# A block-causal attention and gated-MLP kernel: the same program with the work of every engine put in another order

## The chip, the cores and the metric

The kernel runs on one core of a Trainium2 chip, in one launch. The metric is the device time of that launch in microseconds: the median of 3 runs before the change, beside one profiled execution of its own. Engines are named as in the profile: PE is TensorE's matmul (PEld its weight load), DVE VectorE, ACT ScalarE, POOL GpSimd, SP the SyncE queue, which here issues the loads and the regrouping transfers.

## The reference

Attention on 8 images, 8 heads, 576 tokens, head size 64, with a mask that lets a block of 64 tokens see itself and all blocks before it. The heads side by side (512 wide) go through a gated MLP: a projection to 1024 with ReLU, one half normalised per token and mixed over the tokens by a 576 x 576 matrix, multiplied with the other half, and projected to 512.

```python
def _attn_ref(q, k, v):                       # q, k, v: 8, 8, 576, 64
    scores = scale * np.matmul(q, k.transpose(0, 1, 3, 2))
    mask = block_i >= block_j                 # blocks of 64 tokens
    scores = np.where(mask, scores, -1000000000.0)
    scores = scores - np.max(scores, axis=-1, keepdims=True)
    attn = np.exp(scores)
    attn = attn / (np.sum(attn, axis=-1, keepdims=True) + 1e-09)
    return np.matmul(attn, v).astype(np.float32)

def _moe_ref(x, w_in, w_spatial, b_spatial, w_out):   # x: 8, 576, 512
    h = np.maximum(x @ w_in, 0.0)
    u, v = (h[..., :d_ff // 2], h[..., d_ff // 2:])   # 512 each
    v_n = (v - mu) / np.sqrt(var + 1e-06)             # per token
    v_s = np.einsum('ts,bsd->btd', w_spatial, v_n) + b_spatial[None, :, None]
    gated = u * v_s
    return (gated @ w_out).astype(np.float32)
```

## The kernel before

**The program as a list.** The whole program is a string of step words, `ORDER` (line 46 on). A word such as `a.5*2` names a kind of step, its numbers and how often it is taken. `step()` advances the generator of that step until it has issued at least one instruction, and `in_order()` then chains each new instruction behind the last one of its engine. So the string alone sets the order on every engine and on the SP queue; semaphores between engines only follow from the data.

**Attention.** The 8 images have 4 head pairs each, 32 pairs `g` in all; image `b` needs pairs 4b to 4b+3. `load.g` brings queries and keys of a pair into one of two `raw` buffers (576 KB, L373), `loadv.g` the values into one of two `v` buffers. For pairs 4 to 31: `s.g` are the score products (L801 by 512 columns, into three PSUM banks and one shared one, each freed when DVE has read it at L593), `8.g` those of the last 64 rows (L619), `n.g` the softmax's scaling on POOL (L695) and DVE, `t.g` 8 groups of 32 x 32 block transposes on DVE (L849, L839), which fill a buffer `pb`. `r.g` and `r8.g` are four DMA issues each on SP that regroup `pb` into `ptt` (L877, 320 KB; L869, 80 KB). `a.g` is attention times values (L894, L906), ended by evacuations on ACT and DVE (L506, L508) into `x`. Pairs 0 to 3, and a part of pair 4, go another way at the start (`set`, `ns`, `ts`, `alo`, `ahi`: L735 and L763 scores, transposes on TensorE at L453, products at L532 to L558).

**MLP of image b.** `v.b.*` are the products for the mixed half (L947, L959), `u.b.*` for the other half (L1030, evacuated by ACT at L1036), `g.b.*` the token mixing (L1082, L1086, L1087), ended by the multiplication with u on DVE (L1090), and `o.b.*` the last projection, cut into smaller products whose sums DVE and ACT add up (L1162; L1170, L1174 and L1183). These groups share two PSUM banks (pool `ps_m`): a group starts when the evacuation of the one two before it has ended.

**Weights** are fetched on SP and decoded into two parts while pairs 0 to 7 run: `w.k` (512 KB from L238; decode on DVE at L256, L265, L280 and on ACT) and `sw.c` (the token-mixing matrix, 288 KB each at L336). The tail of the program is the MLP of image 7, with no attention left beside it.

Of the kernel before, what the change touches and what calls it, by code (L numbers as in the profile page):

```python
# [47 lines left out]
set.4*2 set.3 ns.3 set.4 ts.1*4 w.0 ns.3 w.0 w.2*2 w.0 set.4 ns.4*2 w.2 w.0 loadv.0 alo.0*2
ts.2*4 set.5 sw.1 set.5 sw.2*4 ts.3*4 set.5*2 set.6 set.5 set.6*4 w.0*2 set.7 alo.0 set.7*2
w.2*2 ns.5*3 set.7*2 ns.6*3 ahi.0 set.7*4 load.2 set.8*3 ts.4*2 ts.5*2 ahi.0 set.8 ns.7*3  # L50
set.10*4 ts.5*2 w.3 ahi.0 ns.7 ts.6*4 set.9*5 ahi.0*2 ts.4*2 w.3*2 ns.8 ts.7*2 ns.7 ts.7*2 w.2*2
ns.8 set.10 ns.9*3 set.11*7 loadv.1 ahi.1*3 set.11*2 ns.10*3 w.3*4 load.3 set.12*2 ahi.1*2 ts.8
pad ts.8 set.12*2 ts.9 sw.0*4 alo.1 ts.9 ts.10*2 set.14*2 w.4*2 ns.11*3 alo.1*2 ts.9*2 ts.10*2
ns.12*2 ts.8*2 set.13 w.4 set.13*4 ns.11*2 w.4 set.14*2 w.5*2 set.14 w.5 loadv.2 ahi.2*3 ns.13*3
w.6*2 set.15*3 ts.11*4 w.5*2 ns.14*3 w.4*2 ahi.2*3 ts.12*4 set.15*6 w.5*2 load.4 set.16 ts.13*2
alo.2*2 ts.13*2 loadv.3 set.16*2 ts.14*4 alo.2 set.16*3 w.4 ns.15*5 sw.4 load.5 set.17*4
set.18*2 ns.16*3 w.6*5 ahi.3*2 set.17 ts.15*3 set.19 ahi.3 ts.15 set.18*2 ahi.1 set.18 set.19*2
alo.3*2 8.5 ns.17*3 sw.1*3 ahi.3*3 w.7 set.19*3 ns.18 set.19*3 alo.3 v.0.0*2 ns.18 sw.4*3 t8.4*2
ns.19*4 t.4*2 v.0.0*2 8.5*2 v.0.1*2 w.8*3 loadv.4 w.7*2 t.4*2 ns.19 v.0.1*2 v.0.2*2 ns.18 t.4*3
ahi.0 t.4 sw.4*2 v.0.0*4 v.0.1*3 w.8 v.0.1 w.7*2 v.0.2*2 v.0.3*2 8.5 w.8*4 8.5*2 v.0.2*3  # L60
u.0.1.0*2 w.7*2 v.0.3*2 s.5 load.6 s.5*9 r8.4 8.5 n.5*2 v.0.4*2 w.9 v.0.3 8.5*2 s.5*5 n.5*4
s.5*2 v.0.4*2 u.0.1.1*2 v.0.2 t8.5*2 n.5 t.5*2 r.4 w.9*4 v.0.4*2 n.5 a.4 n.5*3 t.5*6 a.4*3 w.9*2
8.6*3 u.0.1.3 u.0.0.1*2 sw.3*2 w.9*4 8.6 v.0.3*3 w.9*2 u.0.1.3 a.4*2 w.10*3 u.0.0.0*2 u.0.0.3*2
v.0.4*2 sw.3*2 s.6*4 8.6*2 v.0.4 r8.5 s.6*2 v.0.4*2 loadv.5 w.9*2 u.0.1.2*2 8.6*3 s.6*6 w.10*2
w.9*3 g.0.0.0*4 n.6*3 s.6*5 u.0.0.2*2 t8.6*2 load.7 8.7*3 n.6*8 r.5 a.5*4 w.10*3 t.6*8 w.11*6
loadv.6 g.0.0.1*2 g.0.0.2*2 8.7*3 w.11*3 a.5*2 g.0.0.1*2 w.11*2 g.0.1.1*3 8.7*3 w.11*3 s.7*8
n.7*3 r8.6 g.0.0.3 load.8 8.8 s.7*9 w.11*2 n.7*5 w.11 split.8*2 n.7*3 g.0.0.3 g.0.1.0*4 r.6
a.6*4 t8.7*2 loadv.7 t.7*3 w.11 t.7*5 g.0.1.3*4 split.8 g.0.1.2*3 g.0.1.0*3 g.0.1.1*4 g.0.1.3
a.6 g.0.1.3*2 load.9 g.0.1.3 8.8*4 o.0.0.1*2 a.6 8.8 r8.7 g.0.1.2*3 o.0.0.0*2 s.8*6 8.8*3 s.8*6
g.0.1.2*2 o.0.1.1*3 s.8*5 split.9 o.0.1.0*3 n.8*2 g.0.1.2 t8.8*2 8.9*2 g.0.1.3 r.7 a.7*2 h.0.0*4  # L70
o.0.2.0*2 8.9*2 o.0.2.1*2 o.0.3.0 a.7*3 h.0.1 n.8*2 o.0.4.0 o.0.3.0 o.0.4.0 h.0.1*3 t.8*2
loadv.8 n.8*3 o.0.3.1*2 o.0.4.1*2 a.7 o.0.5.0*3 o.0.6.0*2 r8.8 8.9*2 t.8 n.8 t.8 n.8 t.8 n.8
t.8*2 n.8 t.8 a.6 v.1.0*4 o.0.6.1*2 o.0.5.1*2 a.4 a.7 a.5 v.1.4*2 split.9*2 v.1.0 s.9*2 v.1.0*3
s.9 load.10 s.9*6 o.0.5.1 v.1.4*4 8.9 n.9 8.9*2 n.9*5 v.1.1*2 s.9*8 u.1.0.0*2 8.10 t8.9*2 n.9*5
o.0.6.1 o.0.6.0 split.10*2 r.8 a.8*4 t.9*4 v.1.1*2 t.9*4 u.1.0.1*2 v.1.4*2 8.10*3 loadv.9
v.1.4*3 v.1.2*2 r8.9 split.10 8.10*2 v.1.3*2 a.8*3 v.1.1*4 o.0.4.1 u.1.0.2*2 v.1.3*3 s.10*6
v.1.2*3 s.10*4 8.10*3 n.10*3 v.1.2*3 u.1.0.3*2 s.10*4 t8.10*2 s.10*3 u.1.1.0*2 load.11 8.11 r.9
a.9 8.11 a.9*3 r8.10 8.11*2 n.10*8 t.10*3 u.1.1.1*2 loadv.11 v.1.3*3 u.1.1.2*2 split.11 loadv.10
t.10*5 split.11*2 u.1.1.3*2 a.9*2 g.1.0.0*4 s.11*5 8.11*2 s.11*8 g.1.0.1*2 s.11*4 8.11*3 n.11*3
g.1.0.2*4 g.1.1.0*3 g.1.0.3*4 n.11*8 t8.11*2 load.12 split.12*2 8.12*2 r.10 a.10*3 g.1.0.1 a.10  # L80
g.1.0.1 t.11*8 g.1.1.1*3 split.12 g.1.1.2*6 8.12*4 g.1.1.0 g.1.1.3*4 o.1.0.0*2 g.1.1.2*3
o.1.0.1*2 a.10 g.1.1.3 load.13 g.1.1.3 8.12*2 g.1.1.1 r8.11 h.1.1 o.1.1.1*3 a.10 g.1.1.3*3
o.1.1.0*2 s.12*6 o.1.1.0 8.12 s.12*3 g.1.1.0 o.1.2.0*2 h.1.0*4 s.12*3 n.12*2 o.1.2.1*2 t8.12*2
s.12*5 g.1.1.1 o.1.3.0 n.12*2 h.1.1*2 split.13 t.12*2 r.11 a.11*4 8.13*2 o.1.3.1*2 o.1.3.0
o.1.4.0*2 o.1.4.1*3 h.1.1 r8.12 o.1.6.1 loadv.12 8.13 n.12*3 o.1.5.0*3 8.13*3 n.12*3 t.12*5 n.12
t.12 o.1.5.1*3 a.11 o.1.6.0*2 split.13*2 o.1.6.1 a.11 v.2.0*4 s.13*3 load.14 s.13*6 u.2.0.0*2
split.14 a.9 a.11 a.10 v.2.4*2 v.2.1 8.13*3 8.14 o.1.6.1 n.13*6 o.1.6.0 s.13*6 v.2.0*4 s.13*2
v.2.4*4 v.2.1 r.12 a.12*4 t8.13*2 u.2.0.1*2 n.13*5 loadv.13 r8.13 t.13*8 split.14*2 v.2.1*6
8.14*5 v.2.3*2 a.12*3 v.2.4*2 v.2.2*2 s.14*5 u.2.0.2*2 v.2.2*3 u.2.0.3*2 8.14 n.14 8.14*2 n.14*2
v.2.3*3 v.2.2*2 s.14*10 u.2.1.0*2 s.14*2 u.2.1.1*2 loadv.15 load.15 8.15 t8.14*2 n.14*3 v.2.4*3  # L90
v.2.2 r.13 a.13 8.15 a.13*3 n.14*5 8.15 v.2.3*3 u.2.1.2*2 t.14*3 u.2.1.3*2 t.14*5 a.13*2
split.15 loadv.14 split.15*2 g.2.0.0*4 8.15*6 g.2.0.1*2 s.15*8 r8.14 s.15*3 n.15*3 g.2.0.2*4
s.15*6 g.2.1.0*3 n.15*8 g.2.0.1*2 g.2.0.3*4 t8.15*2 o.1.4.0 load.16 split.16*2 8.16 t.15*8 r.14
a.14*4 8.16 g.2.1.1*3 load.17 split.16 g.2.1.2*6 8.16*4 g.2.1.3 o.2.0.0*2 o.2.0.1*2 a.14 r8.15
g.2.1.3 h.2.1 g.2.1.3*4 g.2.1.2*2 8.16*3 g.2.1.1 o.2.1.1*3 g.2.1.0 g.2.1.3*3 o.2.1.0*2 a.14
g.2.1.1 s.16*6 o.2.1.0 g.2.1.0 s.16*6 o.2.2.1*2 s.16*5 g.2.1.2 o.2.2.0*2 n.16*4 t.16*2 h.2.0*4
o.2.3.1*2 o.2.3.0 r.15 t8.16*2 a.15*5 8.17*2 o.2.3.0 o.2.4.0*2 o.2.4.1*2 loadv.16 h.2.1*3
o.2.5.0*3 o.2.6.1 a.15 n.16*3 r8.16 t.16 n.16 t.16 n.16 t.16 o.2.6.1 n.16 t.16*2 n.16 t.16
split.17*3 o.2.5.1*2 o.2.6.1 o.2.6.0*2 8.17*2 o.2.5.1 a.14 v.3.0*4 8.17*2 s.17*2 load.18 s.17*8
a.13 a.15 v.3.4*2 8.17*3 n.17 u.3.0.0*2 split.18*2 8.18 r.16 a.16 v.3.1 v.3.0*4 v.3.4*4 n.17  # L100
s.17*7 n.17*4 t8.17 8.18 t8.17 load.19 a.16*3 split.18 r8.17 v.3.1 n.17 t.17*3 n.17 t.17 n.17*3
t.17*4 u.3.0.1*2 o.2.6.0 u.3.0.2*2 v.3.1*2 v.3.4*2 v.3.1*4 v.3.2*2 a.16*3 8.18*4 v.3.2*3 v.3.3*2
v.3.4*3 s.18*10 u.3.0.3*2 8.18*2 loadv.17 n.18*3 8.18 n.18*3 u.3.1.0*2 8.19 o.2.4.1 s.18*2
v.3.2*2 v.3.3*3 v.3.2 s.18*2 r.17 a.17 s.18*3 a.17*3 t8.18 8.19 t8.18 u.3.1.2*2 v.3.3*2 n.18*5
u.3.1.3*2 v.3.3 u.3.1.1*2 8.19 t.18*8 a.17*2 r8.18 split.19 loadv.18 split.19*2 g.3.0.0*4 8.19*6
g.3.0.1*2 s.19*8 n.19*3 g.3.0.2*4 s.19*5 g.3.0.1*2 s.19*4 n.19*8 g.3.1.0*3 g.3.0.3*4 t8.19*2
# [1243 lines left out]
```

## Time and profile before

| | |
|---|---|
| median of 3 runs | 646.62 us (646.48 to 647.33) |
| profiled execution | 645.08 us, of which the span of the trace is 643.3 us |
| PE busy | 631.9 us (98%) |
| DVE, POOL, ACT busy | 501.3, 431.2, 423.5 us |
| granted clock of PE | 1.00 in every slice |
| DMA moved | 93.47 MB, 145 GB/s on the mean |

Time stamps below are microseconds from the start of the span. A line of the table of waits says which line of which engine stood idle for which releaser, for how long in total, how often, and the longest one.

### The profile page before, as it was taken

Reading aid. Unit: us, or ns where it says so; the run is one execution under the profiler, and the core shown is the slowest. Engines: PE = TensorE matmul, PEld = TensorE weight load, DVE = VectorE, ACT = ScalarE, POOL = GpSimd, SP = SyncE. Lnnn points to the kernel's source line nnn. Section 1 sums busy time; section 2 is a strip of 40 time slices with the busy share of each in tenths; the row PEclk is TensorE's granted clock in tenths of the full one; section 3 lists DMA queues with packets and bytes.
Section 4 is the critical chain, followed back from the end, with each engine's and each line's share of the span. In section 5 each row is a group of like instructions: output and inputs, shape, how many; then the busy total and the mean of one; then the engine's idle time right before and its main releaser. Section 6 shows DMA issues by size and latency. Waiting matters only on the chain.

```text
span 643.3 us, 15882 instructions
## 1 busy us (share of the span) xinstructions
PE 631.9 (98%) x5380; PEld 548.6 (85%) x5380; DVE 501.3 (78%) x1847; ACT 423.5 (66%) x1214; POOL 431.2 (67%) x690
## 2 busy tenths in 40 slices
...
GB/s 265 195 147 184 158 170 210 142 140 167 143 140 119 206 161 150 136 147 139 126 195 163 156 126 130 183 122 187 163 123 186 121 169 144 134 108 70 1 10 74
DMA packets 51109, 93.47 MB, mean 145 GB/s; under 512 B 5970, under 2 KB 27986, under 8 KB 51028
## 3 DMA queue, kind: packets, MB, share of 16 engines
...
## 4 chain that ended last, share of the span: by engine, by line
PE 84%; DVE 5%; ACT 4%; DMA 3%; SPq 1%; POOL 1%; issue 1%; DVEq 0%; ACTq 0%
PE mu L1030 15%; PE ms L1082 14%; PE mv L947 13%; PE mo L1162 12%; PE av L894 8%; PE s L801 8%; PE s L619 2%; PE av L906 2%; PE mv L959 2%; PE s_first L763 2%; PE t L453 2%; ACT p L598 1%; DMA raw<-qk 1%; PE ms L1087 1%; PE ms L1086 1%
## 5 line engine op out<-in xcount | busy, mean ns | idle before, releaser
L598 ACT ACTIVATE p<-p,sst 128x256 f32<-128x256 f32 (+2 forms) x240 | 131.9, 552 | 19.4 <-DVE sst L593 15.9
L695 POOL TENSOR_SCALAR p<-p,sst 128x512 f32<-128x512 f32 (+4 forms) x244 | 128.1, 544 | 18.7 <-DVE sst L691 9.4
L1030 PE MATMUL mu<-x,wi_hi 128*128 128x288 f32 x512 | 109.7, 299 | 1.1 <-ACT u L1036 1.1
L849 DVE STREAM_TRANSPOSE pb<-p 128x512 f32<-128x512 f32 (+1 forms) x224 | 93.3, 476 | 4.9 <-POOL p L695 4.0
L593 DVE CUSTOM_DVE_ANT_0 p<-s,mask 128x512 f32<-128x512 f32 (+1 forms) x216 | 93.0, 483 | 4.2 <-PE s L801 3.9
L1008 POOL TENSOR_TENSOR vl<-vr,vh 128x512 fp32r<-128x512 f32 x32 | 41.7, 1305 | 73.2 <-ACT vh L1006 62.5
L1030 PEld LDWEIGHTS mu<-x,wi_hi 128*128 128x128 f32 x512 | 84.0, 188 | 4.1 <-ACT u L1036 1.4
L947 PE MATMUL mv<-wi_hi,x 128*128 128x512 f32 x256 | 83.7, 394 | 0.0
L1082 PE MATMUL ms<-ws_hi,vh 128*128 128x288 f32 x256 | 77.4, 302 | 1.4 <-DVE u L1090 1.4
L1082 PE MATMUL ms<-ws_hi,vl 128*128 128x288 f32 x256 | 75.6, 295 | 0.0
L1082 PE MATMUL ms<-ws_lo,vh 128*128 128x288 f32 x256 | 75.5, 295 | 0.0
L894 PEld LDWEIGHTS av<-ptt,v 128*64 128x64 f32 x896 | 53.6, 137 | 21.6 <-issue 10.4
L1030 PE MATMUL mu<-x,wi_lo 128*128 128x288 f32 x256 | 69.7, 294 | 0.0
L894 PE MATMUL av<-ptt,v 128*64 128x64 f32 (+3 forms) x896 | 67.9, 303 | 0.9 <-DMA ptt<-pb 0.9
L947 PEld LDWEIGHTS mv<-wi_hi,x 128*128 128x128 f32 x256 | 48.0, 188 | 10.8 <-issue 0.4
L673 POOL TENSOR_SCALAR p<-p,sst 128x288 f32<-128x288 f32 x56 | 28.3, 516 | 41.0 <-DVE sst L644 27.2
L1090 DVE TENSOR_TENSOR u<-ms,u 128x288 f32<-128x288 f32 x64 | 28.6, 450 | 33.7 <-PE ms L1087 33.5
L1082 PEld LDWEIGHTS ms<-ws_hi,vh 128*128 128x128 f32 x256 | 48.3, 189 | 4.2 <-DVE u L1090 1.6
L947 PE MATMUL mv<-wi_lo,x 128*128 128x512 f32 x128 | 50.0, 391 | 0.0
L1030 PEld LDWEIGHTS mu<-x,wi_lo 128*128 128x128 f32 x256 | 48.1, 188 | 0.6
L1082 PEld LDWEIGHTS ms<-ws_lo,vh 128*128 128x128 f32 x256 | 48.3, 189 | 0.0
L1082 PEld LDWEIGHTS ms<-ws_hi,vl 128*128 128x128 f32 x256 | 48.2, 188 | 0.0
...
## 6 DMA issues: line engine op xcount, KB each, us to landing
...
```

The costliest lines, as they stand in the source:

```text
L593: nc.vector.tensor_tensor_reduce(out=p, in0=ps, in1=mask[:, 512 - ps.shape[1]:], scale=-0.125, scalar=BIG, op0=ALU.add, op1=ALU.min, accum ...
L598: nc.scalar.activation(p, p, AF.Exp, bias=st[:, k:k + 1], scale=-1.0, accum_out=st[:, 10 + k:11 + k])
L695: nc.gpsimd.tensor_scalar(out=p, in0=p, scalar1=st[:, k:k + 1], scalar2=1.0, op0=ALU.mult, op1=ALU.mult)
L801: mm(ps[(t, hd)], q[js, Q_AT[t]:Q_AT[t] + P], k[js, K0:K0 + n], start=(m == 0), stop=(m == len(of) - 1),)
L849: nc.vector.transpose(to(C_AT[hd][0] + 32 * t, dims), p)
L894: mm(to[js, :, 32 * c:], vt[:, c, js], ptt[:, 2 * z:2 * z + 2, at:at + P - 32 * c], start=(c == 0), stop=(c == 3),)
L947: mm(ps, xs[k][:, j, cs], w[:, k, DH:], start=(n == 0), stop=(n == 3 * NC - 1),)
L1008: nc.gpsimd.tensor_tensor(out=vl, in0=vr, in1=vh.bitcast(F32), op=ALU.subtract)
L1030: mm(ps[:, :HT], w[:, k, ds], xs[k][:, j, zs], start=(n == 0), stop=(n == 3 * NC - 1),)
L1082: mm(ps[:, :HT], a[:, ds], w[:, k, zs], start=(n == 0), stop=False)
L1090: nc.vector.tensor_tensor(out=uz, in0=ps[:, :HT], in1=uz, op=ALU.mult)
L1162: mm(ps, y[:, k, es], a[:, k, :], start=(m == 0 and n in (0, 1, 3)), stop=(m == 3 * DQ - 1), skip_group_check=True,)
```

## The change

Only the string `ORDER` is another. Kinds, numbers and counts of the steps are the same, and so are the counts of instructions on every engine; on PE the groups stand at most some 5 us from where they stood, and PE's order is the same in the last 60 us. The first lines of the string:

```diff
--- before.py
+++ after.py
@@ -44,114 +44,114 @@
 ORDER = """
-w.1*7 load.0 set.0*9 set.1*5 ns.0*5 set.2*4 w.0 ns.1*3 set.3*3 set.2 ns.2*3 ts.0*4 load.1
...
+w.1*7 load.0 set.0 sw.2*2 set.0*8 set.1*5 ns.0*5 set.2*5 ns.1*3 w.0*3 set.3*3 ns.2*3 ts.0*4
...
```

Three places follow in the order of the instructions. The first is the SP queue at the start of the program, where `raw_0`, `raw_1`, `raw_2` are queries and keys of pairs 0 to 2, `r_gh`, `r_rw` and `r_gl` weights, `rs` a part of the token-mixing matrix. Before:

```order
L371 DMA raw_0_151<-qk 128x320
L238 DMA r_gh<-w_in 128x4x256
L373 DMA raw_1_229<-qk 128x1152
L238 DMA r_rw<-w_in 128x4x256
L418 DMA v_0_267<-v 128x640
L336 DMA rs_294<-w_spT 128x576
L336 DMA rs_297<-w_spT 128x576
L373 DMA raw_2_364<-qk 128x1152
```

And in the changed program:

```order
L371 DMA raw_0_151<-qk 128x320
L336 DMA rs_165<-w_spT 128x576
L238 DMA r_gh<-w_in 128x4x256
L373 DMA raw_1_234<-qk 128x1152
L418 DMA v_0_264<-v 128x640
L238 DMA r_rw<-w_in 128x4x256
L373 DMA raw_2_310<-qk 128x1152
L238 DMA r_gl<-w_in 128x4x256
```

One part of the token-mixing matrix has moved ahead of the weights and of `raw_1`, the other behind `raw_2`, and the values of pair 0 stand before a weight.

The second place is DVE at about 98 to 103 us: the transposes of pair 6 end, `r_rw` is a weight being decoded, `u` times `ms` is the end of a token-mixing group, `x` times `av` the evacuation of a.5 (pair 5), `sst` the softmax's statistics. Before:

```order
L849 STREAM_TRANSPOSE pb_2_1371<-p_1_2_1_1352 128x4x32
L265 SCALAR_TENSOR_TENSOR r_rw<-r_rw 128x512
L1090 TENSOR_TENSOR u_1000<-ms_0_1_1450,u_1000 128x288
L1090 TENSOR_TENSOR u_1000<-ms_0_2_1466,u_1000 128x288
L631 TENSOR_SCALAR sst_3_1376<-sst_3_1376 64x6
L636 TENSOR_SCALAR sst_3_1376<-sst_3_1376 64x1 x2
L644 TENSOR_SCALAR sst_3_1376<-sst_3_1376 64x6
L280 TENSOR_TENSOR r_rw<-r_rw,r_gl 128x256
L508 TENSOR_TENSOR x_1_1408<-av_1_0_1399,x_1_1408 128x256
L508 TENSOR_TENSOR x_1_1408<-av_1_1_1410,x_1_1408 128x320
L280 TENSOR_TENSOR r_rw<-r_rw 128x256
L1090 TENSOR_TENSOR u_1000<-ms_1_1_1497,u_1000 128x288
```

And in the changed program:

```order
L849 STREAM_TRANSPOSE pb_2_1358<-p_1_2_1_1353 128x4x32
L508 TENSOR_TENSOR x_1_1392<-av_1_0_1383,x_1_1392 128x256
L265 SCALAR_TENSOR_TENSOR r_rw<-r_rw 128x512
L1090 TENSOR_TENSOR u_1025<-ms_0_1_1449,u_1025 128x288
L631 TENSOR_SCALAR sst_3_1365<-sst_3_1365 64x6
L636 TENSOR_SCALAR sst_3_1365<-sst_3_1365 64x1 x2
L644 TENSOR_SCALAR sst_3_1365<-sst_3_1365 64x6
L280 TENSOR_TENSOR r_rw<-r_rw,r_gl 128x256
L508 TENSOR_TENSOR x_1_1392<-av_1_1_1394,x_1_1392 128x320
L1090 TENSOR_TENSOR u_1025<-ms_1_1_1480,u_1025 128x288
L280 TENSOR_TENSOR r_rw<-r_rw 128x256
```

The first evacuation of a.5 stands ahead of the decode, the second where it stood. On PE the row was g.0.0.1, g.0.0.2, g.0.1.1, s.7 (16 score products), g.0.0.3, and is now g.0.0.1, g.0.1.1, s.7, g.0.0.2.

The third place is DVE at about 433 to 436 us, where `o` times `mo` is a sum of the last projection of image 4, `x` times `av` the evacuation of a.23, and `pb` the first transposes of pair 24. Before:

```order
L631 TENSOR_SCALAR sst_1_6439<-sst_1_6439 64x6
L636 TENSOR_SCALAR sst_1_6439<-sst_1_6439 64x1 x2
L644 TENSOR_SCALAR sst_1_6439<-sst_1_6439 64x6
L508 TENSOR_TENSOR x_3_6461<-av_3_0_6452,x_3_6461 128x256
L508 TENSOR_TENSOR x_3_6461<-av_3_1_6463,x_3_6461 128x320
L1183 TENSOR_TENSOR o_3_0_6485<-mo_0_0_6277,o_3_0_6485 128x288
L849 STREAM_TRANSPOSE pb_0_6431<-p_6_0_0_6367 128x4x4x32
```

And in the changed program:

```order
L690 TENSOR_SCALAR sst_0_6154<-sst_0_6154 128x12
L691 RECIPROCAL sst_0_6154<-sst_0_6154 128x4
L1183 TENSOR_TENSOR o_3_0_6482<-mo_0_0_6285,o_3_0_6482 128x288
L652 ISA p_99,sst_1_6426<-s_6_1_1_6428,mask 128x288
L652 ISA sst_1_6426 128x1
L631 TENSOR_SCALAR sst_1_6426<-sst_1_6426 64x6
L636 TENSOR_SCALAR sst_1_6426<-sst_1_6426 64x1 x2
L644 TENSOR_SCALAR sst_1_6426<-sst_1_6426 64x6
L849 STREAM_TRANSPOSE pb_0_6393<-p_6_0_0_6362 128x4x4x32
```

The sum of `o` stands ahead of the second read of pair 25's scores and of the three statistics, and the two evacuations `x` have moved behind all the transposes of pair 24.

At the end of the attention work (565 to 582 us) PE takes the last attention product, a.31, three groups of the last projection (o.6.2.0, o.6.2.1, o.6.3.0) later, and a.30 one group of token mixing (g.6.0.3) earlier; SP issues the 320 KB of r.31 before the 80 KB of r8.31, which was the other way round; on DVE the 8 transposes of t.31 stand ahead of the multiplication that ends g.6.0.3. Of the 28 attention products a.4 to a.31, 12 stand earlier on PE against the groups around them, by 0.2 to 2.0 us of work, 10 later by 0.65 to 3 us, and 6 where they were.

## Rows read from the trace of the kernel before

**Rows 1.** The page's busy times, share of the span, instructions.

```profile
PE 631.9 (98%) x5380; PEld 548.6 (85%) x5380; DVE 501.3 (78%) x1847; ACT 423.5 (66%) x1214; POOL 431.2 (67%) x690
```

**Rows 2.** Waits of PE: total, times, longest.

```profile
PE ms L1082 <- DVE u L1090: 1.4, 1, 1.4
PE mu L1030 <- ACT u L1036: 1.1, 1, 1.1
...
PE av L894 <- DMA ptt<-pb: 0.9, 1, 0.9
PE s L619 <- DVE sst L593: 0.6, 1, 0.6
PE mo L1162 <- ACT s L1174: 0.6, 1, 0.6
...
PE mo L1162 <- DVE o L1183: 0.5, 1, 0.5
```

**Rows 3.** Busy us by engine, the sum over windows of 58 to 136 us.

```profile
sum 78.00, PE 73.97 PEld 62.90 DVE 70.02 ACT 55.35 POOL 70.66; mean PE 5.69 PEld 4.84 DVE 5.39 ACT 4.26 POOL 5.44
```

**Rows 4.** The SP queue's timeline from the start: start us, us, instruction.

```profile
3.69 0.51 SPq L373 DMA_DIRECT2D raw<-qk  x1
...
5.67 2.19 SPq L336 DMA_DIRECT2D rs<-w_spT  x2
```

**Rows 5.** Line L373 at 3.69 us, its issue to landing.

```profile
DMA to landing us min/median/max: 7.6/7.6/7.6
```

**Rows 6.** PE's timeline at the start, idle before in brackets.

```profile
11.78 1.19 PE L735 MATMUL s_first<-raw 64*64 64x288 f32 x8
...
37.54 1.84 PE L549 MATMUL av<-pthi,v 128*64 128x320 f32 x12 [0.22 <-DVE sst L690]
```

**Rows 7.** One window, 4 to 10 us: busy us, then PEclk, DMA share, GB/s.

```profile
4.00:10.00 6.00, 5.32 (x28) 3.20 (x27) 4.19 (x19) 4.24 (x14) 1.81 (x3) 1.00 0.97 324
```

**Rows 8.** DVE's timeline at 98 to 103 us.

```profile
98.62 1.19 DVE L265 SCALAR_TENSOR_TENSOR r_rw<-r_rw 128x512 int32<-128x512 int32 x1
99.74 0.81 DVE L1090 TENSOR_TENSOR u<-ms,u 128x288 f32<-128x288 f32 x2
...
101.83 0.81 DVE L508 TENSOR_TENSOR x<-av,x 128x256 fp32r<-128x256 f32 x2
```

**Rows 9.** PE's timeline at 102 to 105 us.

```profile
102.30 2.43 PE L801 MATMUL s<-raw 64*128 64x512 f32 x16
104.65 0.40 PE L1082 MATMUL ms<-ws_hi,vh 128*128 128x288 f32 x1
```

**Rows 10.** The chain of waits at 137 us: start us, us, what.

```profile
137.57 1.60 PE mo L1162 x12
```

**Rows 11.** DVE's timeline at 434 us.

```profile
434.04 0.82 DVE L508 TENSOR_TENSOR x<-av,x 128x256 fp32r<-128x256 f32 x2 [0.29 <-ACT x L506]
434.78 0.45 DVE L1183 TENSOR_TENSOR o<-mo,o 128x288 f32<-128x288 f32 x1
```

**Rows 12.** The chain of waits at 570 to 578 us.

```profile
570.90 5.59 DMA ptt<-pb
...
576.63 1.31 PE av L894 x16
```

**Rows 13.** DVE's timeline at 565 to 571 us.

```profile
565.10 3.22 DVE L849 STREAM_TRANSPOSE pb<-p 128x512 f32<-128x512 f32 x8
568.86 0.46 DVE L1090 TENSOR_TENSOR u<-ms,u 128x288 f32<-128x288 f32 x1 [0.54 <-PE ms L1087]
570.70 0.46 DVE L1090 TENSOR_TENSOR u<-ms,u 128x288 f32<-128x288 f32 x1 [1.39 <-PE ms L1087]
```

**Rows 14.** Line L877 at 345 to 349 us: durations in ns, first and last start.

```profile
L877 SPq DMA_DIRECT2D ptt<-pb x4: 555/1365/2254, 344.9 to 348.3; - x4
...
DMA to landing us min/median/max: 4.9/6.4/7.2
```

**Rows 15.** PE's timeline at 354 us, the start of a.19.

```profile
354.42 2.40 PE L894 MATMUL av<-ptt,v 128*64 128x256 f32 x32
```

More of the change, by code (lines that the diff above doesn't have):

```diff
@@ L46 @@
 ORDER = """
-w.1*7 load.0 set.0*9 set.1*5 ns.0*5 set.2*4 w.0 ns.1*3 set.3*3 set.2 ns.2*3 ts.0*4 load.1
[L48 to L106, printed above, removed]
```

155 lines of the change are left out of this document (107 added, 48 removed).

## The prediction

> **What bounds the kernel now.** I read the busy times first: PE is busy for 631.9 us, 98% of the span, and no other engine for more than 78% [rows 1]. The same products run after the change, at a granted clock that was already at its top, so only PE's idle time can go, 11.4 us of 643.3. Next the table of PE's waits [rows 2]. The reader is to see there that every line occurs once: these are single places, not a rhythm. Those that an order can touch are, where I found them in the timeline: 1.4 us for a multiplication on DVE (at 100.24, g.0.1.1), 1.1 us for ACT (at 80.21), 0.9 us for a regrouping transfer (at 576.63, a.31), 0.6 us for DVE (at 107.38), 0.6 us for ACT (at 130.53, o.0.4.0), 0.5 us for DVE (at 435.28, o.4.5.0). With a few small ones that is some 5.4 us. The rest is the start before the first data and the tail, which the change leaves as they are.
>
> Then the windows from 58 to 136 us, in which the first MLP groups, the weights' decode and the first full attention pairs meet: DVE is busy for 70.0 and POOL for 70.7 of 78 us [rows 3]. In that stretch PE, with 74.0, has 4 us of its idle time, and a place that DVE frees there for one instruction is taken by the next.
>
> The change is told place by place, since what does not wait on PE costs nothing in this kernel.
>
> **The start.** raw_1 was issued at 3.69 us [rows 4], took 7.6 us to land [rows 5], thus 11.29, and PE first needs it at 11.78 [rows 6]: 0.49 us to spare. Now one part of the token-mixing matrix stands ahead of it on SP, 128 x 576 words of 4 bytes, 0.295 MB. At the 324 GB/s that moved there, with the DMA engines 0.97 busy [rows 7], that is 0.91 us; its issue takes 1.1 us of SP, half of 2.19 [rows 4]. Both delays run at once, so the bounds are 0 (the transfers share the engines and raw_1 was not held) and 1.1 us, and I take 0.9, because the engines are full: a wait of 0.4 us.
> The Trainium skill, "DMA: Bandwidth & Descriptors", section on queues, rings and completion order, says that each DMA engine takes its descriptors in the order of its ring. That speaks against this edit: the matrix part would hold up raw_1 by its whole transfer, and not by a share; the trace of before shows no such pair of transfers the other way round, so it does not decide. By the rule the wait of 0.4 us is certain, and a start without it, which would bring the sum below to -1.8, falls away.
> Against it stands the weight decode that DVE did just before PE's wait of 0.22 us at 37.54 [rows 6] and of another 0.28 us at 44.93; it has moved some 7 us forward. I let 0.3 of the 0.5 go. The start: +0.1 (between -0.5 and +0.6).
>
> **58 to 113 us.** The wait of 1.4 us for the multiplication goes away where it was, since g.0.1.1 now follows g.0.0.1 directly and its bank is long free. What is late next are the score products of s.7 behind it. They would begin at about 98.9, and after four of their groups need the bank that the second evacuation of a.5 frees. On DVE that evacuation keeps its place: before, the two of 0.4 us began at 101.83, 3.2 us after the decode's start at 98.62 [rows 8]. Now one has moved ahead of the decode and one multiplication (half of 0.81) has left the row, so the second begins at 98.62 + 0.40 + 3.21 - 0.40 = 101.8 and ends at 102.2. PE comes to it at about 100.3 and waits 1.9 us, does what is left of s.7 (a third of 2.43 [rows 9]) until 103.0, then g.0.0.2 in 1.9, the length that g.0.1.1 had: 104.9, where before the same four pieces were done at 104.65 [rows 9]. So +0.25 there. ACT's and DVE's waits at 80.21 and 107.38 lie on rows of DVE that hardly change between 66 and 98 us; small gaps around them may give the 0.25 back. I take 0 for the stretch, between -3.1 (1.4 + 1.1 + 0.6 all gone) and +1.4 (one more such wait).
>
> **130 us.** o.0.4.0 waited 0.6 us for a copy on ACT [rows 2]. Now another group of the last projection, o.0.3.1, stands before it. Two such groups took 1.60 us [rows 10], so one takes 0.8, more than the wait. -0.6 (between -0.9, if a second small gap there closes, and 0, if ACT does its next piece first).
>
> **435 us.** o.4.5.0 waited 0.5 us for a sum on DVE that started at 434.78, behind three statistics and the two evacuations of a.23, 0.82 us, which themselves stood 0.29 idle for ACT [rows 11]. Now the sum stands ahead of all of these. -0.5 (between -0.7 and 0).
>
> **560 to 582 us.** a.31 waited 0.9 us for its regrouping transfer, which took 5.59 us and ended at 576.49, the last thing of the chain [rows 12]. Now it comes behind three groups of the projection, 3 x 0.8 = 2.4 us of work, less 1.9 us because a.30 moved forward by one group; and SP issues the large transfer ahead of the small ones, so that it starts earlier. The wait goes. Its rival is made on DVE: the eight transposes of t.31, 3.22 us, ended at 568.32, and the multiplication behind them stood idle 0.54 [rows 13], so they have room; but now one more multiplication (0.46), the evacuations of a.30 (0.81), the short transposes (0.80) and again a multiplication (0.46) follow: 568.32 + 0.46 + 0.81 + 0.80 + 0.46 = 570.85. The groups there come every 570.70 - 568.86 = 1.84 us [rows 13], and PE would want that bank at about 570.6: 0.3 us late. -0.9 + 0.3 = -0.6 (between -0.9 and +0.1).
>
> **Products nearer to their transfers.** Of the 28 products a.4 to a.31, 12 stand earlier, by 1.7, 1.1, 0.6, 0.2, 1.7, 0.8, 0.9, 0.6, 0.9, 0.2, 0.6 and 2.0 us. An example shows what they had to spare: r.19's last issue was at 348.3, the quickest landing there took 4.9 us [rows 14], and a.19 began at 354.42 without waiting [rows 15]: between 0 and 1.2 us. It now comes 0.9 us earlier. Only one of the 28 waited in this profile [rows 2]. I take +0.2 for all of them, between 0 and +3.5 (a spare of 0.8 us each, worked out below).
>
> **The sum.** +0.1 + 0 - 0.6 - 0.5 - 0.6 + 0.2 = -1.4 us: 645.08 to 643.7 for the profiled execution. That one was 1.54 us quicker than the median of the runs, 646.62, so the median becomes 645.2 us.
>
> **The rivals.**
> *DVE and POOL set the pace, and waits only change their place.* For it: 58 to 136 us, where at s.7 a wait of 1.4 is paid for with one of 1.9; the same would hold at 435 and 570, where DVE's work is pushed from one side of a PE wait to the other. Against it: after 136 us PE's idle time is under 4 us in 450, so there is slack around most waits. Its time: the three gains of 1.7 are halved to 0.85, and the start and the regrouping cost 0.3 and 0.2: -0.35, 646.3 us.
> *The whole stretch 58 to 113 us comes free as well.* For it: the first evacuation of a.5 leaves earlier, and every decode that moves out of DVE's way there shortens a row that was full. Against it: the row that counts ends where it did. Its time: half to all of the 3.1 us more, -1.4 - 2.7 = -4.1: 642.5 us.
> *The products wait for their transfers: slower.* The mechanism is the regrouping of pairs, 320 KB behind 4 issues of SP, landing after a product wants it. Its price is the sum, over the 12 products, of how much further each moved than it had to spare. With 0.8 us to spare each: 0.9 + 0.3 + 0.9 + 0.1 + 0.1 + 1.2 = 3.5 us, less the gains of 1.6, is +1.9: 648.5 us. With 1.0 us it is 2.5, and the total +0.9, no difference. So it decides from a mean spare below some 0.9 us, which is within what a.19 showed. Against it: 27 of 28 products did not wait, and SP's issues have moved too, some of them forward as r.31.
>
> **How the numbers follow.** A difference under 0.2%, 1.3 us, can't be told from none by a measurement of this kernel. The forecast, a gain of 0.7 to 2.5 us, has 0.45: 0.36 of it beyond 1.3 us and 0.09 within. All of 58 to 113 us gone: 0.10, faster. The pace of DVE and POOL: 0.27, of which 0.26 within and 0.01 faster. Slower through the transfers: 0.18, and there I also put the ends of the start and of 58 to 113 us, which are worth up to 2 us together. Together 0.47 faster, 0.35 the same, 0.18 slower. The forecast's own range is 644.1 to 645.9. The range for 8 in 10 leaves out some of the fastest and of the slowest cases: 642.9 to 647.6.
>
> **What would show it.** Right: in PE's waits no line at a.31, none at o.0.4.0 and o.4.5.0; at s.7 a wait of 1.5 to 2 us for DVE's L508 in place of the 1.4 for L1090; a small wait for raw at about 11.8 us. Wrong: waits of PE for `ptt` that sum to over 2 us; or, in 58 to 113 us, PE's idle time below 1 us, which would put the time nearer to 642.5.

## The result, and the profile after

The changed kernel takes 639.75 us (639.42 to 640.71, 4 runs) against 646.55 us for the kernel before (645.10 to 647.33, 4 runs): a ratio of 0.990, 95% interval 0.9879 to 0.992. In the later series before stood at 645.25 to 645.73 us, and the changed kernel, run once more, at 639.64 (ratio 0.9912, 0.9899 to 0.9926). The forecast said faster, 645.2 us, with a range down to 642.9: the direction is right, the size is less than a quarter of what came, and the time lies outside the range.

The profiled execution has a span of 638.9 us instead of 643.3. PE's line of busy times after (answers to [rows 1]):

```profile
PE 629.6 (99%) x5380; PEld 547.2 (86%) x5380; DVE 501.3 (78%) x1847; ACT 424.4 (66%) x1214; POOL 428.6 (67%) x690
```

The same 5380 matmuls count 2.3 us less as busy, and idle time falls from 11.4 to 9.3 us. So half of the gain of this profile never stood in the idle column. PE's waits after (line, releaser, total, times, longest; answers to [rows 2]):

```profile
PE s L801 <- DVE x L508: 1.7, 2, 1.0
PE s_first L763 <- DMA raw<-qk: 1.4, 2, 1.1
PE warm L208 <- DVE mask L202: 1.1, 1, 1.1
PE mu L1030 <- ACT u L1036: 0.6, 1, 0.6
PE t L453 <- POOL p L695: 0.5, 1, 0.5
PE ms L1082 <- DVE u L1090: 0.4, 1, 0.4
PE s_first L619 <- DMA raw<-qk: 0.3, 1, 0.3
```

No line is left at a.31, o.0.4.0 or o.4.5.0. Two new waits for L508 stand at s.6 and s.7. Between 58 and 113 us PE is idle for 2.8 us (0.6, 0.7, 1.0 and 0.4), where it was 3.1 before (1.1, 1.4 and 0.6).

Where the time went is read by one rule: both orders reach the same set of groups at some places on PE, and the start of the next group there can be subtracted. The table gives the time between such places. "Before" is the profile shown ahead and a second one of the same order; "after" likewise; the last column is the forecast of the stretch.

| from the first matmul of | to | before | after | difference | forecast |
|---|---|---|---|---|---|
| (span's start) | set.4 | 11.78, 11.82 | 12.53, 11.45 | +0.75, -0.37 | +0.4 |
| set.4 | v.0.0 | 41.60, 41.57 | 40.67, 40.39 | -0.93, -1.18 | -0.3 |
| v.0.0 | v.1.0 | 81.28, 81.33 | 79.41, 79.42 | -1.87, -1.91 | -0.6 |
| v.1.0 | g.4.0.2 | 265.87, 265.81 | 265.68, 265.80 | -0.19, -0.01 | +0.2 |
| g.4.0.2 | v.5.0 | 38.07, 38.13 | 37.25, 37.24 | -0.82, -0.89 | -0.5 |
| v.5.0 | g.6.0.0 | 113.62, 113.60 | 113.57, 113.61 | -0.05, 0.01 | 0 |
| g.6.0.0 | v.7.0 | 34.21, 34.41 | 33.02, 33.03 | -1.19, -1.38 | -0.6 |
| v.7.0 | last group | 52.70, 52.67 | 52.66, 52.66 | 0 | 0 |
| sum | | | | -4.35, -5.74 | -1.4 |

The first line varies with the arrival of the first loads, from 11.2 to 12.5 us over all the profiles taken, under either order; the other lines repeat within 0.3 us here. The second pair is the fairer one. The start, the stretch behind it up to 135 us, and the two late places carry all. Between 58 and 136 us PE is busy for 75.2 us after, DVE and POOL for as much as before and a little more (answers to [rows 3]):

```profile
sum 78.00, PE 75.22 PEld 63.78 DVE 70.78 ACT 55.01 POOL 71.26; mean PE 5.79 PEld 4.91 DVE 5.44 ACT 4.23 POOL 5.48
```

**The start.** The SP queue after (answers to [rows 4]) and raw_1's landing (answers to [rows 5]):

```profile
3.21 0.43 SPq L336 DMA_DIRECT2D rs<-w_spT  x1
3.69 0.43 SPq L238 DMA_DIRECT2D r_gh<-w_in  x1
4.16 0.50 SPq L373 DMA_DIRECT2D raw<-qk  x1
```

```profile
DMA to landing us min/median/max: 7.8/7.8/7.8
```

The issue of `rs` costs 0.43 us and not the 1.1 taken from a pair; raw_1 lands at 4.16 + 7.8 = 11.96, 0.67 us later than before, and PE comes to it at 12.53 because its first loads were late. No wait for raw_1 follows. Over the profiles taken, raw_1 landed at 10.0 to 11.3 us with the old start (eight profiles) and at 10.7 to 12.0 us with `rs` ahead of it (six), 0.66 us later on the mean, of which 0.47 is its later issue.

**At 98 us.** DVE after (answers to [rows 8]), then PE at s.7 (answers to [rows 9]):

```profile
98.11 0.39 DVE L508 TENSOR_TENSOR x<-av,x 128x256 fp32r<-128x256 f32 x1
98.42 0.90 DVE L265 SCALAR_TENSOR_TENSOR r_rw<-r_rw 128x512 int32<-128x512 int32 x1
...
101.34 0.48 DVE L508 TENSOR_TENSOR x<-av,x 128x320 fp32r<-128x320 f32 x1
```

```profile
99.16 1.77 PE L801 MATMUL s<-raw 64*128 64x512 f32 x8
101.96 0.92 PE L801 MATMUL s<-raw 64*128 64x256 f32 x8 [1.03 <-DVE x L508]
```

The mechanism is the one forecast, with 1.03 us in place of 1.9 (and 0.27 more inside s.7, which takes 2.63 us without its wait where it took 2.36): PE came to the bank at 100.93 and not at 100.3, and the evacuation ended at 101.8 and not at 102.2, since the decode began 0.2 us earlier and took 0.90 instead of 1.19.

**At 107 us** the forecast left a wait where it was, but 8.8 had moved. PE's rows for the eight matmuls of 8.8, before and after:

```profile
107.38 1.19 PE L619 MATMUL s<-raw 64*64 64x288 f32 x8 [0.60 <-DVE sst L593]
```

```profile
112.21 0.72 PE L619 MATMUL s<-raw 64*64 64x288 f32 x8
```

The wait of 0.60 is gone, and the group is 0.47 us shorter as well: three of its eight matmuls began at 107.85 and the last three at 108.15, the first of these just behind DVE's next read (L593), which ended at 107.80. The row counts such a wait as busy.

**At 118 us** the forecast has no term, but the order is another there too. Before, the second evacuation of a.6 on DVE stood behind the reads and the statistics of 8.8, and s.8 waited for it:

```profile
119.81 0.49 DVE L508 TENSOR_TENSOR x<-av,x 128x320 fp32r<-128x320 f32 x1
```

```profile
120.45 0.41 PE L801 MATMUL s<-hi 64*128 64x384 f32 x1 [0.33 <-DVE x L508]
```

In the changed order both evacuations stand ahead of them (from the second profile):

```profile
114.64 0.81 DVE L508 TENSOR_TENSOR x<-av,x 128x256 fp32r<-128x256 f32 x2
```

s.8 takes 2.7 us from its first matmul to the next group in the profiles with the old order at this place, and 2.0 in those with the new one, with the start of either kernel (e2_start against e4_58 below). Where both orders have done the same matmuls, the line from v.0.0 to v.1.0 can be cut further; both pairs of profiles give the same to 0.1 us: +0.2 up to 104.9 us, -0.65 from there to 113.5 us (8.8), -0.76 to 122 us (s.8), and -0.7 to v.1.0 (o.0.4.0).

**At 432 and 570 us.** DVE's sum of o.4.4.0 after (answers to [rows 11]) follows 0.96 us of idle time in which DVE waits for PE, and no wait of PE for it is left; the chain of waits after (answers to [rows 12]) has no transfer any more:

```profile
431.70 0.46 DVE L1183 TENSOR_TENSOR o<-mo,o 128x288 f32<-128x288 f32 x1 [0.96 <-PE mo L1162]
```

```profile
569.41 5.69 PE mo L1162 x42
575.10 2.33 PE av L894 x32
```

And DVE at 562 to 566 us (answers to [rows 13]); the last of the transposes of t.31 end at 563.82, the multiplications follow without a wait of PE:

```profile
562.53 1.29 DVE L849 STREAM_TRANSPOSE pb<-p 128x128 f32<-128x128 f32 x4 [0.67 <-POOL p L695]
563.90 0.46 DVE L1090 TENSOR_TENSOR u<-ms,u 128x288 f32<-128x288 f32 x1
...
565.82 0.42 DVE L1090 TENSOR_TENSOR u<-ms,u 128x288 f32<-128x288 f32 x1
```

### The profile page after: what moved, and what is told of

Read it like the earlier page. It is cut to its first block, busy times and chain, and to the rows that moved or that the text cites. A ratio compares the mean times of both kernels' runs of the same rounds, so it can differ in the third digit from the quotient of the medians.

```text
span 638.9 us, 15873 instructions
## 1 busy us (share of the span) xinstructions
PE 629.6 (99%) x5380; PEld 547.2 (86%) x5380; DVE 501.3 (78%) x1847; ACT 424.4 (66%) x1214; POOL 428.6 (67%) x690
## 4 chain that ended last, share of the span: by engine, by line
PE 87%; DVE 7%; DMA 2%; ACT 1%; POOL 1%; issue 1%; SPq 0%; DVEq 0%; POOLq 0%
PE ms L1082 15%; PE mo L1162 15%; PE mu L1030 14%; PE mv L947 12%; PE av L894 10%; PE s L801 7%; PE s L619 2%; PE av L906 2%; PE mv L959 2%; DMA raw<-qk 2%; DVE p L593 2%; PE t L453 1%; PE ms L1087 1%; PE ms L1086 1%; PE s_first L763 1%
## 5 line engine op out<-in xcount | busy, mean ns | idle before, releaser
L598 ACT ACTIVATE p<-p,sst 128x256 f32<-128x256 f32 (+2 forms) x240 | 132.1, 553 | 14.4 <-DVE sst L593 10.7
L695 POOL TENSOR_SCALAR p<-p,sst 128x256 f32<-128x256 f32 (+4 forms) x244 | 128.0, 543 | 18.3 <-DVE sst L691 4.8
L593 DVE CUSTOM_DVE_ANT_0 p<-s,mask 128x512 f32<-128x512 f32 (+1 forms) x216 | 92.9, 483 | 3.6 <-PE s L801 3.2
L947 PEld LDWEIGHTS mv<-wi_hi,x 128*128 128x128 f32 x256 | 48.1, 188 | 10.7 <-issue 0.4
L1062 POOL TENSOR_TENSOR a<-u,a 128x288 fp32r<-128x288 f32 x48 | 38.6, 808 | 27.6 <-ACT a L1058 25.1
L1090 DVE TENSOR_TENSOR u<-ms,u 128x288 f32<-128x288 f32 x64 | 28.8, 451 | 28.8 <-PE ms L1087 23.8
```

The source lines that it names most:

```text
L593: nc.vector.tensor_tensor_reduce(out=p, in0=ps, in1=mask[:, 512 - ps.shape[1]:], scale=-0.125, scalar=BIG, op0=ALU.add, op1=ALU.min, accum ...
L598: nc.scalar.activation(p, p, AF.Exp, bias=st[:, k:k + 1], scale=-1.0, accum_out=st[:, 10 + k:11 + k])
L695: nc.gpsimd.tensor_scalar(out=p, in0=p, scalar1=st[:, k:k + 1], scalar2=1.0, op0=ALU.mult, op1=ALU.mult)
L947: mm(ps, xs[k][:, j, cs], w[:, k, DH:], start=(n == 0), stop=(n == 3 * NC - 1),)
L1062: engine.tensor_tensor(out=lo, in0=f, in1=hi.bitcast(F32), op=ALU.subtract)
```

## The experiments

Hybrids take the steps of one string up to a place and the rest in the order of the other. The theories: W, the gain is that of PE's waits, those hidden in groups that take longer than their like included; P, DVE and POOL set the pace of 58 to 136 us; R, the moved attention products and their transfers carry it; L, the profiled execution of before was a lucky one.

### The order of before again

The kernel unchanged.

> The kernel before once more, under another name: how far two builds of one order stand apart, and a second profile of it. Theory L (the profiled execution of before, 645.1 against 646.6 to 647.3 us for its other runs, was only a lucky one): the second profile shows waits of PE within 1 us of the first, and its own time lies above 646. Theory R (in most executions regrouping transfers land later than in the one profiled): PE's waits for ptt sum to 1.5 us or more in the second profile, at other products than a.31. Both: a ratio of 1.000 within 0.002.

645.26 us against 645.25, ratio 1.000 (0.9991 to 1.0009), the profiled execution 645.26. The table of waits repeats; only the transfer at a.31 differs, 1.1 us instead of 0.9:

```profile
PE av L894 <- DMA ptt<-pb: 1.1, 1, 1.1
```

So R falls, and L too in its plain form: executions and profile agree. The 1.5 us that I added to come from the profiled execution to the median belong to the first series; why before was 1.3 us slower there, and the changed kernel not, stays open.

### The changed order in one part: up to 135, 135 to 412, from 412 us

```diff
 ORDER, steps ahead of the first v.1.0 (some 135 us):
-  as before
+  as in the changed string; all others in the order of before
```

> The changed order up to the first products of v.1.0 (some 135 us), the order of before from there. The two profiles put 2.05 us of the whole 4.35 here, of which the forecast had 0.5 to 0.6. Theory W (the gain is that of the waits in the profile, those hidden inside stretched groups included): 2 us quicker in the trace, -2 to -3 us in the runs. Theory R (the moved attention products and their transfers carry it): under 1.5 us in the runs.

643.08 us, ratio 0.9963 (0.9951 to 0.9976), -2.2 us. By the places of the table -1.18 from set.4 to v.0.0 and -1.93 from there to v.1.0, as in the whole change. Later 0.7 is given back, since a.31 in the order of before waits 1.8 us:

```profile
PE av L894 <- DMA ptt<-pb: 1.8, 1, 1.8
```

That wait is not steady: 0.9 to 1.8 us in seven profiles with this order of the end. W fits.

```diff
 ORDER, steps of 135 to 412 us:
-  as before
+  as in the changed string
```

> The order of before, but the changed one for the work that lies between 135 and 412 us. There PE shows no idle time of its own in either profile, and the two traces differ by only 0.2 us. Theory W: no difference, -0.2 us (within 0.5). Theory R: -2 us or more, since 16 of the 28 attention products that moved lie here. The forecast: +0.1 to +0.2.

645.80 us, ratio 1.0007 (0.9998 to 1.0016). The trace shows a new wait of 0.55 us behind the seam and a longer one at o.0.4.0 (1.25), so that the hybrid says only that no gain of 2 us lies here. R falls again.

```diff
 ORDER, steps from 412 us:
-  as before
+  as in the changed string
```

> The order of before up to some 412 us, the changed one from there. The two profiles put 2.1 us here: 0.9 at 432 to 436 us and 1.2 at 560 to 582 us, where the forecast had 0.5 and 0.6. Theory W: -2 to -2.5 us. The forecast: -1.1. Theory R: between the two, since 8 attention products lie here.

645.72 us, ratio 1.001 (1.000 to 1.002): a miss of every theory, by a seam. The first group behind it waits for a multiplication (lines of this kernel are numbered one higher):

```profile
PE mo L1163 <- DVE u L1091: 2.3, 1, 2.3
```

2.3 us were lost there and 2.3 won later. Four of the 11 runs have a mean granted clock of 0.997 and took 646.8 to 647.6 us; the seven at 1.000 took 645.0 to 645.8. A seam in a schedule has a price of its own, and only the trace tells it apart.

### The changed kernel again, its start alone, three moves alone, its second half alone

> The changed kernel once more, beside the order of before on the same chip. By the traces (theory W, waits) it should be 4.4 us quicker, and up to 1 us more where the first load does not come as late as in the first profile of it (PE began 0.23 us later there and waited 1.05 us at 7.72): -4.4 to -5.4 us, 640 to 641 us if before stands at 645.3. If -6.8 us is the real size, 638.5, and something that no trace shows gives the rest.

639.64 us against 645.73, ratio 0.9912 (0.9899 to 0.9926), -6.1 us; the trace -5.8 (637.7 against 643.5 us).

```diff
 ORDER, steps ahead of the first v.0.0 (some 53 us):
-  as before
+  as in the changed string
```

> The changed order up to the first products of v.0.0 (some 53 us), the order of before from there. My forecast had +0.1 us for this part. Theory W: -1.0 us at 53 us in the trace, as in the kernel that has the changed order up to 135 us, and it stays until the end: -1.0. Theory P (DVE and POOL set the pace of 58 to 136 us, my rival): what is gained at 53 us is waited for at 80 to 131 us again: 0.0 at 135 us and in the runs.

Run e2_start: 642.71 us, ratio 0.9957 (0.9945 to 0.997), -3.0 us; the trace -2.4. By the table -1.16 between set.4 and v.0.0, and, with the order of before from there on, another -1.01 between v.0.0 and v.1.0. P is wrong here: the gain is not waited for again, it grows. The growth is at two places: u.0.0.0 waits 0.86 instead of 1.13, and o.0.4.0 does not wait at all. The second is a matter of ACT. There an output's DMA issue stands ahead of the copy that o.0.4.0 waits for; ACT's queue before, and in this kernel:

```profile
124.84 2.17 ACTq L1186 DMA_DIRECT2D outT<-o  x1
```

```profile
123.17 0.38 ACTq L1186 DMA_DIRECT2D outT<-o  x1
```

Over the kernels measured with o.0.4.0 in its old place, an issue of 2.16 to 2.22 us went with a wait of 0.58 to 0.67, one of 2.70 and 2.81 with 1.13 and 1.25, and one of 0.38 with none. What holds the issue back was not tried.

```diff
-... r8.6 g.0.0.3 load.8 8.8 s.7*9 ... r.6 a.6*4 t8.7*2 ...
+... r8.6 g.0.0.3 load.8 s.7*9 ... r.6 a.6*4 8.8 t8.7*2 ...
-... n.8*2 o.0.4.0 o.0.3.0 o.0.4.0 ... n.8*3 o.0.3.1*2 ...
+... n.8*2 o.0.3.1 o.0.4.0 o.0.3.0 o.0.4.0 ... n.8*3 o.0.3.1 ...
-... o.6.0.1*2 r8.31 a.30 ... o.5.4.1 r.31 a.31*2 ...
+... o.6.0.1*2 r.31 a.30 ... o.5.4.1 r8.31 a.31*2 ...
```

> The order of before with three moves alone: the first products of 8.8 (PE) four groups later, behind the first half of a.6; o.0.3.1 ahead of o.0.4.0; on SP the four large issues r.31 ahead of the four small r8.31. Theory W, for each in the trace: -1.07 us at 113 us (0.60 of idle time and 0.47 inside the group, which takes 1.12 where its like takes 0.65); -0.6 at 131 us; -0.9 to -1.1 at 577 us. Together -2.6 in the trace, -2.5 in the runs. Theory P: the first moves the wait to g.0.1.0 or a.6, 0 at 113 us. For the third, the rival is that the transfers and not the order of their issue are late: then under 0.3 of its 0.9 goes.

Run e2_moves: 643.37 us, ratio 0.9968 (0.9955 to 0.998), -2.4 us. In the trace, against the second profile of before: the order of the two groups of SP's issues takes the wait at a.31 away, -1.14 between g.6.0.0 and v.7.0, so it is this row that did it. Between v.0.0 and v.1.0 only -0.66, the 0.6 of o.0.4.0: the 1.07 that 8.8 gave were there at 113 us and were waited for again by 122, at o.0.0.1 and o.0.1.1:

```profile
PE mo L1162 <- POOL a L1062: 0.4, 1, 0.4
...
PE mo L1162 <- DVE u L1090: 0.3, 1, 0.3
```

Here P is right: a wait taken away alone moves on. In this kernel s.8 still takes 2.70 us; in the whole change, where s.8 is short as well, what 8.8 gives stays.

```diff
 ORDER, steps from some 250 us:
-  as before
+  as in the changed string
```

> The order of before up to some 250 us, the changed one from there; the seam is at a place where both have done nearly the same steps. Theory W: -2.2 to -2.6 us in the trace (0.4 at 290 to 300 us, 0.9 at 432 to 436, 1.2 at 560 to 582) and as much in the runs. My forecast had -1.1. A value near 0 would say that these waits go only together with the changed start.

642.36 us, ratio 0.9958 (0.9944 to 0.9972), -3.4 us; the trace -3.0, of which 0.88 between g.4.0.2 and v.5.0 and 1.39 between g.6.0.0 and v.7.0. W holds at these two places. Another 0.6 lies between v.1.0 and g.4.0.2, where the whole change gains nothing; that is not explained.

### One place, one wait: 435 us, the first loads, and a try for more

```diff
-8.25*2 a.23*6 o.4.3.0 o.4.4.0*2 o.4.3.1*2
+8.25*2 a.23*3 o.4.3.0 o.4.4.0*2 a.23*3 o.4.3.1*2
```

> The order of before, with the second copy on ACT and both evacuations on DVE of a.23 behind the sum of o.4.4.0. My forecast: the wait of 0.5 us at 435 goes and no more. Theory W, with the time hidden inside o.4.4.0 and o.4.3.1 (1.01 and 0.96 where such a group takes 0.80): -0.8 to -0.87 us in the trace at 436 us. The copy on ACT alone, or DVE's transposes behind it, could keep a part: -0.5.

This kernel was profiled once and its time was not measured beside before. In the trace -0.77 from g.4.0.2 to v.5.0 (37.36 against 38.13): the wait at o.4.5.0 and the length hidden in the two groups ahead of it. The whole change has -0.89.

```diff
-w.1*7 load.0 set.0 sw.2*2 set.0*8 ... ts.0*4 load.1 ...
+w.1*7 load.0 set.0*9 ... ts.0*4 load.1 sw.2*2 ...
```

> The changed kernel with the first part of the token-mixing matrix fetched behind raw_1 again, as before. My forecast charged its place ahead of raw_1 with 0.4 us (a wait of PE at 11.5 us, 0.26 in the second profile of the changed kernel). If that is the price: no wait for raw_1 and -0.3 us at 13 us, and the same saving in the runs, unless the matrix part now comes too late for its split and takes it back by 20 us.

640.41 us, ratio 0.9912 (0.9898 to 0.9927), the ratio of the changed kernel. The first loads came so late in this profile (PE at set.1 at 7.64 us, after 1.44 of waiting) that it tells nothing of raw_1. The wait of 0.26 that I took for raw_1's stands in the table of that profile as one for DVE. So that term, if there is one, is smaller than the runs can tell.

```diff
-v.0.4*2 r.4 loadv.4 a.4*4 n.5*3 ... 8.6*2 w.9*4 u.0.1.3*2 8.6*3 u.0.0.1*2 sw.3*2 w.9*4 a.4*2
+v.0.4 r.4 loadv.4 a.4*3 u.0.1.3*2 a.4 v.0.4 n.5*3 ... 8.6*2 a.4*2 w.9*4 u.0.0.1*2 8.6*3 sw.3*2 w.9*4
-a.5*2 w.11*4 w.10*3 ... 8.7*2 w.11*3 a.5 g.0.1.1*2 ... g.0.0.1 s.7*9 g.0.0.2*2
+a.5*2 w.11*3 a.5 w.11 w.10*3 ... 8.7*2 w.11*3 g.0.1.1*2 ... g.0.0.1 s.7 g.0.0.2*2 s.7*8
```

> The changed kernel with six moves of single instructions ahead of the waits that its profile still shows between 74 and 108 us (0.59 for ACT at u.0.0.0, 0.74 for an evacuation at s.6, 1.03 at s.7, 0.44 at g.0.0.3, and some 0.27 inside each of s.6 and s.7): ACT evacuates u.0.1.3 and u.0.0.1 ahead of small steps and exponentials; DVE evacuates a.4 ahead of a decode and statistics, and the second half of a.5 ahead of the 1.1 us decode; g.0.0.2 ends ahead of the reads of s.7. Theory W (each wait hangs on the order of one row): 2 to 3.3 us less in the trace at 113 us, 636.5 to 637.5 us against 639.6. Theory P (DVE and POOL set the pace there): the waits come back at the next group, under 0.8 us less at 135 us, 639 to 640.

645.66 us, as slow as before (ratio 0.9998). All four waits are gone, two new ones for ACT (0.3 and 0.6) stand at 84 and 87 us, and PE is 1.5 us ahead at 105 us, but at s.8 it waits as long as nowhere else:

```profile
PE s L801 <- DVE lo L387: 4.0, 1, 4.0
```

DVE's row for that subtraction, and POOL's rows beside it (start us, us):

```profile
113.66 5.85 DVE L387 TENSOR_TENSOR lo<-raw,hi 128x512 fp32r<-128x512 f32 x1
```

```profile
113.44 1.01 POOL L387 TENSOR_TENSOR lo<-raw,hi 128x384 fp32r<-128x384 f32 x1
114.41 0.81 POOL L1120 TENSOR_TENSOR s<-u 128x288 f32<-128x288 f32 x1
115.17 0.80 POOL L1062 TENSOR_TENSOR dl<-u,dh 128x288 fp32r<-128x288 f32 x1
...
118.18 0.79 POOL L1123 TENSOR_TENSOR u<-s,u 128x288 f32<-128x288 f32 x1
122.30 0.80 POOL L1120 TENSOR_TENSOR s<-u 128x288 f32<-128x288 f32 x1 [3.33 <-DVE u L1090]
```

The same instruction took 0.68 us in the second profile of the changed kernel, where POOL was idle for 0.33 us when it began. Seven two-input operations of POOL stand without a gap here, and DVE's ends half a microsecond after the last of them.

The wait of 4.0 us is not its whole price. Ahead of s.8 PE is 1.1 us in front of the changed kernel and behind the group that follows 5.3 us back, 6.4 us in all. The other 2.4 are the clock: the granted clock of PE was 1.00 (2.4 GHz) up to 116 us, PE stood idle from 115.56 to 119.57, and the clock was 0.50 (1.2 GHz) from 118 to 124 us and 1.00 again from 126 us. The page shows it in its eighth slice (112.5 to 128.6 us):

```profile
PEclk9999999799999999999999999999999999999999
```

The page of the changed kernel has no such slice, and all 12 runs of this one have a mean granted clock of 0.995 or 0.997.

```diff
-t.7*5 split.8 t.7*3 g.0.1.3*3 ... g.0.1.1*4 split.8 o.0.0.1*2
+t.7*5 split.8*2 t.7*3 g.0.1.3*3 ... g.0.1.1*4 o.0.0.1*2
```

> The changed kernel with the six moves of the run before that removed the waits of 74 to 108 us, and one more: DVE's subtraction for pair 8 (L387, 128x512) now comes behind the fifth of its eight transposes, ahead of the multiplication of g.0.1.3. In the run before it took 5.85 us instead of 0.68, exactly as long as POOL worked through six two-input operations without a gap, and PE waited 4.0 us for it at s.8. Theory C (a two-input operation of DVE cannot run beside those of POOL and is held until POOL has a gap): at its new place it starts beside POOL's scalings, takes 0.7 to 1.7 us, the wait at s.8 goes, and the kernel is 1.0 to 1.6 us quicker than the changed one at 113 us and at the end: 638.2 to 638.9 where the changed one has 639.6. Theory D (the 5.85 us come from its data, raw_8 or hi landing late): it is as long here, the wait stays, and the time is 645 again.

639.34 us, ratio 0.9904 (0.9889 to 0.9919). What theory C forecast came: the subtraction takes 0.65 us beside POOL's scalings, and the wait at s.8 is gone; theory D falls.

```profile
112.34 0.65 DVE L387 TENSOR_TENSOR lo<-raw,hi 128x512 fp32r<-128x512 f32 x1
```

```profile
110.58 2.65 POOL L695 TENSOR_SCALAR p<-p,sst 128x384 f32<-128x384 f32 x5
```

PE's idle time between matmuls up to 600 us falls from 4.5 us in the second profile of the changed kernel to 2.4, but of the 1.9 us won at 105 us only 0.7 are left at v.1.0 (78.73 against 79.42 us from v.0.0), and the runs can't tell the kernel from the changed one. Theory P again, for the larger part.

```diff
 ORDER, steps of 53 to 135 us:
-  as before
+  as in the changed string
```

> The order of before, with the changed one for the work between 53 and 135 us only. Forecast for this stretch: 0 at 58 to 113 us and -0.6 at 130. Theory W: the differences of the other hybrids, -3.02 less -1.2 to -1.4 us, so -1.5 to -1.8 in the trace at 135 us, of which 0.6 is o.0.4.0. Theory P (DVE and POOL set the pace): -0.6 alone, since the move of 8.8 by itself gave 1.07 at 113 us and was waited for again by 122 us.

Run e4_58: 645.10 us, ratio 0.9992 (0.9983 to 1.0001). From v.0.0 to v.1.0 81.25 us, no gain, but 1.2 us of it are lost at the seam (0.91 in one wait at 62.5 us). Behind it, up to 105 us, this order loses 0.8 us where the whole change loses 0.2; from 105 us to v.1.0 it wins 2.1 us, as the whole change does. So the gain at 8.8, s.8 and o.0.4.0 does not need the changed start, and between 62 and 105 us the start is worth some 0.6 us, if nothing of that is the seam's.

## Why the prediction was wrong

Two steps failed. The sum was made up of waits that stand in the table of PE's waits, and half of the gain was in groups that wait in their middle; and the changed places at the start and at 107 to 122 us, which gave 2.6 of the 5.7 us of the second pair of profiles, stood in it with 0.3.

- **What bounds the kernel**: half right. PE's idle time was named as all that can go; 2.3 of the 4.4 us in the first pair of profiles were stretched groups, which a table of waits does not hold. So the "some 5.4 us" of waits that an order can touch were no upper bound; the second pair has 5.7.
- **The start, +0.1**: failed. Measured -0.9 and -1.2 between set.4 and v.0.0, where 0.3 was granted for two visible waits of 0.5. From 37.5 us to 44.9 us the changed start needs 0.8 us less, and two thirds of that have no idle row in the trace of before. One decode on DVE, just ahead of the first of these waits, took more than twice as long there as its like four microseconds on. POOL was busy with two-input operations beside it, up to 36.61 us, and the decode ended 0.28 us later (rows of DVE and POOL before):

```profile
35.86 1.03 DVE L256 TENSOR_SCALAR r_gl<-r_gl 128x512 int32<-128x512 int32 x1
...
40.21 0.43 DVE L256 TENSOR_SCALAR r_rw<-r_rw 128x512 int32<-128x512 int32 x1
```

```profile
35.06 1.55 POOL L326 TENSOR_TENSOR ws_lo<-rs,ws_hi 128x288 fp32r<-128x288 f32 x2 [0.31 <-ACT ws_hi L321]
```

  All eight profiles with the old start have this one decode at 1.03 us; in the seven with the changed start none takes over 0.45, and PE has no wait between 36 and 46 us in e2_start. No run moved the decode alone, so how much of the 0.8 us is its work stays open. The start also reaches further: it shortened the wait at u.0.0.0 (1.1 to 0.9) and took away the one at o.0.4.0 (e2_start, -1.0 behind 53 us), which the sum held at 0. The charge for `rs` ahead of raw_1 (0.9 us of delay, and a wait of 0.4 that was called certain) was some 0.7 of delay, and no wait that raw_1 ended.
- **58 to 113 us, 0**: the part that was worked out held. The wait at s.7 came, 1.3 us for 1.9, and at 104.9 us the changed order stood 0.2 us back, where 0.25 was forecast. What failed is the sentence that "ACT's and DVE's waits at 80.21 and 107.38 lie on rows of DVE that hardly change": PE's own row had changed, 8.8 had gone four groups back, and with it went 0.65 us. That move alone gives nothing in the end (e2_moves).
- **113 to 130 us**: no term at all, and -0.76 us. The evacuation of a.6 had changed places on DVE, and the wait of 0.3 at s.8 can only have been among the "few small ones", which no term takes up.
- **130 us, -0.6**: the size was right, 0.6 alone (e2_moves), but there was luck in it: the wait also goes without this move where ACT's DMA issue takes 0.38 us instead of 2.2 (e2_start), and it takes 0.37 in both profiles of the changed kernel.
- **435 us, -0.5**: right in the mechanism, 0.77 alone, 0.89 in the change; the sum left out the 0.37 hidden in two groups of 1.01 and 0.96 us, where others take 0.80.
- **560 to 582 us, -0.6**: right in the mechanism, 1.2 to 1.4. The 0.3 charged for DVE did not come: the transposes of t.31 ended at 563.82, and PE has no wait for the multiplications behind them. And the transfer's wait was 0.9 in the one profile I had, 1.1 in the next.
- **Products nearer to their transfers, +0.2**: 0 in the trace. The slower rival did not occur: no wait for `ptt` is left in either profile of the changed kernel.
- **From the trace to the median, +1.5**: not a property of the kernel; a second profile agreed with its runs. Of the 6.8 us of the first result, 1.3 lie in before being slower in that series, which stays open.
- **The rivals**: the time came beyond the fastest, "the whole stretch 58 to 113 us comes free as well", 642.5, and not by its way: the sign named for it, under 1 us of idle time there, did not come (2.8 us). Pace (P) is real where one wait is removed alone, and not where the start hands the stretch more or where the next place is freed too.
